# Sliding-window attention and a sentence-level expert layer on one core: gate logits inside the third scores tile, the fallback's transfers on GpSimd, the last output tiles on ScalarE

## The chip, the cores and the metric

The kernel runs on one core of a Trainium2 chip. The core has five engines, each with an instruction stream of its own: TensorE (PE in the profile; its weight loads are shown apart as PEld), VectorE (DVE), ScalarE (ACT), GpSimd (POOL) and SyncE (SP). They meet only through semaphores. Transfers (DMA) are issued from SP, ACT or POOL and run on 16 DMA engines that all queues share; those issued from POOL also change the number type on the way. TensorE writes into PSUM, from which ACT and DVE copy results to the on-chip memory.

The metric is the device time of one launch in microseconds (us), and the number that counts is the median of several runs.

## The reference

Two stages, 8 batches, 8 heads, 576 positions, head size 64, 8 experts of 512 x 1024:

```python
# attention: q, k, v of shape (8, 8, 576, 64)
scores = scale * np.matmul(q, k.transpose(0, 1, 3, 2))
rel = pos[:, None] - pos[None, :]
scores = np.where((rel >= 0) & (rel < 64), scores, -1e9)
attn = np.exp(scores - np.max(scores, axis=-1, keepdims=True))
attn = attn / (np.sum(attn, axis=-1, keepdims=True) + 1e-09)
attn_out = np.matmul(attn, v)
# expert layer on x = attn_out, heads side by side: (8, 576, 512)
logits = x.mean(axis=1) @ w_gate            # one row of 8 logits per batch
e_idx = np.argmax(logits, axis=1)           # one expert per batch
gate_w = softmax(logits)[arange(B), e_idx]
out[b] = gate_w[b] * (np.maximum(x[b] @ w1[e_idx[b]], 0) @ w2[e_idx[b]])
```

Every batch is sent to one expert as a whole, and which one is known only when the whole attention output of that batch has been averaged over its positions. Only then can that expert's weights (2 MB each for w1 and w2 in float32, stored as float16 on chip) be fetched.

## The kernel before

The attention work is cut into 16 units `u` of four heads (two per batch). For a unit, q and k are loaded (`load_qk`, on POOL), turned by TensorE (`transpose_qk`), and the scores are made in three pieces `c` (`scores`: 14 small matmuls at L374 into a PSUM tile `sp`, then one exponential on ACT at L389 into `pt`, then one multiplication with the window's mask on DVE, `mask_out`, L396). `values` multiplies with v (L417), whose two float16 copies `va` and `vb` are made on DVE by `cast_part`: "whole" is the cast of v, "low" and "high" are two shifted copies. The normalised result is `x`; `transpose_x` turns it into `xT` and sums it over positions for the gate.

`gate(b)` runs when batch b's two units are done: a small float32 matmul gives the logits (tile `gl`, L494), and a chain on DVE (copy to `glog`, largest value, its index, clamp to `eidx`, `gnm`) gives the expert's number. POOL loads it into a register (L514) and issues the transfer of w1 (`load_w1`, tile `w1t`, L546) and w2 (`load_w2`, `w2t`, L552). `gate_weight(b)` computes the gate's softmax weight on ACT and DVE.

The expert layer of an older batch runs between: `expert_up` (eight matmuls per tile, L574, tile `php`; ACT writes the ReLU to `hT`, L578) and `expert_down` (L588 for four blocks of 128 rows, L605 for the last 64 rows, tile `pso`; a copy into `ob`, then the transfer to `out`).

All PSUM tiles come from one pool with four buffers of two banks, taken in turn: whoever takes a tile waits until the readers of the tile four before it are done. The order of the work is the order in which the program is written; nothing is reordered. The main loop runs over steps `t` (one unit each, with the expert work of an older batch between its parts, dealt out by `experts(pace)`). At even steps a gate runs. From step 8 on these are called `easy`. At an easy step the order is: scores pieces 0 and 1, some expert work, the cast of v for the next unit, more expert work, gate and weight loads, scores piece 2, `gate_weight`, then the shifted copies of v.

SP issues the transfers of v and of nearly all outputs. At the end, the last block of 128 rows of the last batch is split in two halves: DVE copies one (L594, sent by SP, L596), ACT the other (L595, sent by ACT, L597). The 64-row block of the same batch stands just before it (L611, two transfers by SP, L613).

Behind all that, L886 loads a flag on each of the five engines. If a check of the softmax sums failed, `general` recomputes everything in a slower, safer way; with the inputs here it never runs, so every engine branches over its code (L888) to the closing semaphore waits and the barrier (L916). The branch stands in each engine's own stream, so what an engine has to skip is what `general` would do on that engine. On the path that skips it, each engine also waits for, and advances, the semaphores that `general` would have used.

Of the kernel before, what the change touches and what calls it, by code (L numbers as in the profile page):

```python
# [17 lines left out]
def general(nc, tc, const, psum, vpool, wpool, xpool, xtp, hpool, opool, small, ident,  # L18
# [16 lines left out]
    with tc.For_i(0, B, 1) as bi:  # L35
# [3 lines left out]
        for h in range(H):  # L39
            ld = vpool.tile([128, 4, NST, D], FP32, tag="vn", name="gld")  # L40
            for i, src in enumerate((q, k, v)):
                rows = src[sl, h].squeeze(0)
                nc.sync.dma_start(out=ld[:, i, 0:4, :], in_=rows[0:512].rearrange(
                    "(m p) d -> p m d", p=128))
                nc.sync.dma_start(out=ld[0:64, i, 4, :], in_=rows[512:576])
            nc.sync.dma_start(
                out=ld[0:64, 3, 0:4, :],
# [96 lines left out]
        for m in range(NST):  # L144
            n = 128 if m < 4 else 64
            pso = psum.tile([128, 2, 512], FP32, tag="ps", name="gpso")
            for fb in range(FB):
                nc.tensor.matmul(out=pso[0:n, 0, :], lhsT=hT[:, fb, 128 * m:128 * m + n],
                                 rhs=w2t[:, fb, :], start=(fb == 0), stop=(fb == FB - 1))
            ob = opool.tile([128, Dm], FP32, tag="ob", name="gob")  # L150
            nc.vector.tensor_copy(out=ob[0:n], in_=pso[0:n, 0, :])
            nc.sync.dma_start(out=out[sl, 128 * m:128 * m + n, :].squeeze(0),
                              in_=ob[0:n])
# [3 lines left out]
def kernel(  # L157
# [10 lines left out]
    nc = tc.nc  # L168
# [185 lines left out]

    sp_ps = {}

    def add_outside(u, c):

        sp = psum.tile([128, 2, 512], FP32, tag="ps", name="sp")
        for s in range(2):  # L360
            P(nc.tensor.matmul(
                out=sp[:, s, 0:384], lhsT=ident,
                rhs=outside[:, c].rearrange("p g w -> p (g w)"), start=True, stop=False))
        sp_ps[u, c] = sp

    def scores(u, c, mask=True):
        qT, kT = qt_tiles[u], kt_tiles[u]
        masked = (u, c) in sp_ps
# [16 lines left out]
        for g in range(g0, g0 + 6):  # L385
            for s in range(2):
                mm(s, g % 2, g, g, 128 if g < g0 + 5 else 64)
        pt = ptp.tile([128, 2, 384], FP16, tag="pt")
        P(nc.scalar.activation(out=pt, in_=sp[:, :, 0:384], func=AF.Exp, scale=scale))  # L389
        pt_tiles[u, c] = pt  # L390
        if mask and not masked:
            mask_out(u, c)
# [98 lines left out]

    def gate(b):
        gl = psum.tile([128, 2, 512], FP32, tag="ps", name="gl")
        P(nc.tensor.matmul(out=gl[:, 0, 0:E], lhsT=onesf, rhs=gparts[b],  # L494
# [87 lines left out]
    def expert_down(b, mt):  # L582
# [3 lines left out]
        if mt < 4:  # L586
# [4 lines left out]
            if b == B - 1 and mt == 3:  # L591

                oc = opool.tile([128, Dm], FP32, tag="ob", name="oc")
                P(nc.vector.tensor_copy(out=ob[:, 0:256], in_=pso[:, 0, 0:256]))  # L594
                P(nc.scalar.copy(out=oc[:, 0:256], in_=pso[:, 0, 256:512]))  # L595
# [5 lines left out]
        else:  # L601

            for fb in range(FB):
                for hf in range(2):
# [5 lines left out]
                        tile_position=(0, 64 * hf)))  # L610
            P(nc.vector.tensor_copy(out=ob[:, 0:256], in_=pso[:, 0, 0:256]))  # L611
            for hf in range(2):
                P(nc.sync.dma_start(  # L613
                    out=out[b, 512:576, ts(hf, 256)],
# [175 lines left out]
    for t in range(START + 1, NU + LAG):  # L790
# [3 lines left out]
        def next_gate():  # L794
            b = t // 2 - 1
            gate(b)
            load_w1(b)
# [25 lines left out]
        if easy:  # L823
            if ahead:
                cast_part(t + 1, "whole")
            experts(pace)
        if gated:

# [9 lines left out]
        if ahead and t > 5:  # L838
            if gated and not easy:
                cast_part(t + 1, "whole")  # L840
        if not easy:
            experts(pace)
        if on:
            scores(t, 2)
        if gated and on:
# [75 lines left out]
```

## Time and profile before

| | |
|---|---|
| runs | 219.78, 220.29, 221.03 us, median 220.29 us |
| profiled execution | 223.27 us, of which the span from the first to the last instruction is 221.6 us |
| PE busy | 199.5 us (90% of the span) |
| ACT busy, DVE busy, POOL busy | 135.0, 127.1, 40.5 us |
| chain that ended last, by engine | PE 52%, DMA 23%, ACT 12%, DVE 5%, issue 3% |
| moved by DMA | 45.64 MB, mean 206 GB/s |
| TensorE clock granted | 0.982 of full speed over the span |

The profile is taken of one execution, which is longer than the median of the runs. In its rows an engine name with a q (SPq, ACTq, DVEq) is that engine's sequencer: branches, semaphore waits, transfers issued. The bracket at a row's end is the idle time of the engine before it and what ended it. A transfer's DMA share is the mean busy share of the 16 DMA engines, counted over packets, so it can exceed 1 a little.

### The profile page before, as it was taken

To read this page: it belongs to the slowest core of one execution; us is meant where nothing else is said; L and a number is where in the kernel's file an instruction comes from. 1 tells how busy PE (TensorE), PEld (TensorE's weight loads), DVE (VectorE), ACT (ScalarE), POOL (GpSimd) and SP (SyncE) were. 2 spreads that over 40 slices of the span, in tenths; PEclk is the share of its full clock that TensorE was granted. 3 is DMA by queue.
4 is the path that set the end of the run, shared out by engine and by line. 5 is a ranking of instruction groups with operands and counts; after the bars stand their busy time and mean duration, and the time that the engine had idled before them with its cause. 6 is when DMAs were issued, how large, how long until landed. Compare 5 with 4: busy or idle time off the path is not lost.

```text
span 221.6 us, 7005 instructions
## 1 busy us (share of the span) xinstructions
PE 199.5 (90%) x3015; PEld 141.1 (64%) x3018; DVE 127.1 (57%) x308; ACT 135.0 (61%) x222; POOL 40.5 (18%) x70
## 2 busy tenths in 40 slices
PE   7668879999899999999799999999999999999940
PEld 2346657756686768855686568774887579469420
DVE  2437698557876867384737576676749473330120
ACT  2277596964768667957588476957593838217200
POOL 7080182053000900052000700050002000200000
PEclk9997999999999999999999999999999999999996
DMA  5999999999999999999999999999955991798240
GB/s 66 238 247 242 181 128 207 242 247 246 234 229 246 305 230 233 239 291 225 242 231 289 179 234 238 245 259 242 247 138 73 219 263 44 122 237 234 82 137 11
DMA packets 32406, 45.64 MB, mean 206 GB/s; under 512 B 2544, under 2 KB 24816, under 8 KB 32368
## 3 DMA queue, kind: packets, MB, share of 16 engines
q0 software_dynamic: 16192, 26.22, 66.7%
q1 hardware_dynamic: 15232, 18.75, 27.6%
q8 instruction: 25, 0.41, 0.7%
q10 hardware_dynamic: 944, 0.16, 0.4%
q14 instruction: 13, 0.11, 0.2%
HBM read 61.90 MB, written 9.44 MB: 322 GB/s over the span
## 4 chain that ended last, share of the span: by engine, by line
PE 52%; DMA 23%; ACT 12%; DVE 5%; issue 3%; POOL 1%; POOLq 0%; ACTq 0%
PE php L574 24%; DMA w1t<-in_moe_w_dram 18%; PE pso L588 13%; PE tp L334 6%; DMA kn<-in_k_dram 5%; ACT pt L389 4%; ACT xT L462 4%; PE op L417 4%; ACT hT L578 3%; PE pso L605 2%; PE sp L374 1%; PE tp L454 1%; DVE pt L396 1%; DVE va L303 1%; PE gl L494 1%
## 5 line engine op out<-in xcount | busy, mean ns | idle before, releaser
L574 PE MATMUL php<-xT,w1t 128*128 128x288 f16 x512 | 69.6, 287 | 3.8 <-DMA w1t<-in_moe_w_dram 2.6
L578 ACT ACTIVATE hT<-php,gatew 128x576 f16<-128x576 f32 x64 | 46.9, 746 | 28.4 <-PE php L574 28.4
L574 PEld LDWEIGHTS <-w1t 128*128 128x128 f16 x512 | 54.9, 113 | 11.9 <-DMA w1t<-in_moe_w_dram 3.9
L588 PE MATMUL pso<-w2t,hT 128*128 128x512 f16 x256 | 60.2, 380 | 0.5 <-ACT hT L578 0.5
L389 ACT ACTIVATE pt<-sp 128x768 f16<-128x768 f32 x48 | 36.6, 822 | 7.1 <-PE sp L374 7.1
L588 PEld LDWEIGHTS <-hT 128*128 128x128 f16 x256 | 23.3, 98 | 26.6 <-issue 1.7
L303 DVE COPY ob<-pso 128x512 f32<-128x512 f32 x23 | 15.9, 690 | 21.6 <-PE pso L588 21.4
L433 DVE TENSOR_TENSOR x<-op,linv 128x640 f16<-128x640 f32 x32 | 26.4, 825 | 1.1
L396 DVE TENSOR_TENSOR pt<-pt,masks 128x768 f16<-128x768 f16 x42 | 23.0, 556 | 6.3 <-ACT pt L389 5.2
L347 ACT COPY dst<-tp 128x1152 bf16<-128x1152 bf16 x16 | 18.0, 1123 | 10.1 <-PE tp L334 9.9
L462 ACT ACTIVATE xT<-tp 128x576 f16<-128x576 f16 x28 | 17.9, 646 | 8.8 <-PE tp L454 8.8
L546 POOL DMA_DIRECT2D w1t<-in_moe_w_dram x5 | 3.6, 718 | 98.0 <-DVE gatew L525 58.6
L417 PE MATMUL op<-vb,pt 128*64 128x65 f16 x320 | 16.4, 198 | 1.0 <-ACT pt L389 0.5
L417 PEld LDWEIGHTS <-pt 128*64 128x64 f16 x640 | 14.0, 114 | 3.9 <-issue 1.9
L417 PE MATMUL op<-va,pt 128*64 128x65 f16 x320 | 16.2, 198 | 0.0
L374 PE MATMUL sp<-dst 64*64 64x128 bf16 (+1 forms) x672 | 13.8, 213 | 2.1 <-ACT dst L301 0.8
L303 DVE COPY vb<-va 64x1152 f16<-64x1152 f16 (+1 forms) x32 | 15.0, 468 | 0.8 <-ACT va L301 0.3
L486 DVE SCALAR_TENSOR_TENSOR gpart<-wg,pooled,gpart 128x8 f32<-128x8 f32 x21 | 4.8, 227 | 18.2 <-ACT xT L462 18.0
L374 PEld LDWEIGHTS <-dst 64*64 64x64 bf16 x672 | 10.3, 107 | 7.3 <-issue 3.0
L303 DVE CAST va<-vn 128x1152 f16<-128x1152 f32 x15 | 11.6, 776 | 4.9 <-DMA vn<-in_v_dram 4.9
L303 DVE COPY dst<-tp 128x1152 bf16<-128x1152 bf16 x8 | 10.9, 1356 | 4.7 <-PE tp L334 4.6
L544 POOL DMA_DIRECT2D w1t<-in_moe_w_dram x7 | 5.6, 800 | 43.5 <-PE pso L588 20.5
(79 smaller groups left out, 185.5 us busy)
## 6 DMA issues: line engine op xcount, KB each, us to landing
w2t<-in_moe_w_dram POOLq DMA_DIRECT2D x8, 1024.0 KB, 17.2
out_dram<-ob SPq DMA_DIRECT2D x31, 256.0 KB, 8.1
w1t<-in_moe_w_dram POOLq DMA_DIRECT2D x5, 1024.0 KB, 8.7
qn<-in_q_dram POOLq DMA_DIRECT2D x16, 288.0 KB, 13.8
kn<-in_k_dram POOLq DMA_DIRECT2D x16, 288.0 KB, 15.4
w1t<-in_moe_w_dram POOLq DMA_DIRECT2D x5, 512.0 KB, 11.1
out_dram<-ob SPq DMA_DIRECT2D x16, 64.0 KB, 7.6
w1t<-in_moe_w_dram POOLq DMA_DIRECT2D x2, 256.0 KB, 4.4
```

The lines of the kernel that those rows point to most:

```text
L303: P(eng.tensor_copy(out=out, in_=in_))
L334: P(nc.tensor.transpose(out=tp[64 * s:64 * s + 64, ts(t, 128)], in_=src[:, s, ts(t, D)], identity=ident, tile_position=(0, 64 * s)))
L347: P(nc.scalar.copy(out=dst.rearrange("p (x r t) -> p x r t", x=2, t=NT), in_=view))
L374: P(nc.tensor.matmul(out=sp[64 * half:64 * half + 64, s, 64 * (qblk - 6 * c):64 * (qblk - 6 * c) + n], lhsT=kT[64 * s:64 * s + 64, ts(kblk ...
L389: P(nc.scalar.activation(out=pt, in_=sp[:, :, 0:384], func=AF.Exp, scale=scale))
L396: P(nc.vector.tensor_tensor(out=pt, in0=pt, in1=masks[:, c].rearrange("p s g w -> p s (g w)"), op=ALU.mult))
L417: P(nc.tensor.matmul(out=op[64 * half:64 * half + 64, xx, 65 * jj:65 * jj + 65], lhsT=pt[:, s, 64 * (g % 6):64 * (g % 6) + 64], rhs=win, s ...
L433: P(nc.vector.tensor_tensor(out=x[:, :, h0 * D:(h0 + 2) * D].rearrange("p j (x c) -> p x j c", x=2), in0=view[:, :, :, 0:64], in1=li[:, :, ...
L462: P(nc.scalar.activation(out=xT[:, kb, :], in_=tp[:, kl, 0:S], func=AF.Copy, accum_out=pooled[:, b, kb:kb + 1]))
L574: P(nc.tensor.matmul(out=php[:, sc, 0:288], lhsT=w1t[:, kb, cols], rhs=xT[:, kb, ts(sc, 288)], start=(kb == 0), stop=(kb == KB - 1)))
L578: P(nc.scalar.activation(out=hT[:, ft].rearrange("p (sc s) -> p sc s", sc=2), in_=php[:, :, 0:288], func=AF.Relu, scale=gatew[:, b:b + 1]))
L588: P(nc.tensor.matmul(out=pso[:, 0, :], lhsT=hT[:, fb, ts(mt, 128)], rhs=w2t[:, fb, :], start=(fb == 0), stop=(fb == FB - 1)))
```

## The change

There are four edits.

1. In `general`, all transfers of inputs and outputs are issued from GpSimd instead of SyncE. SP's code to be skipped shrinks from 186 instructions to 37 and POOL's grows from 44 to 189 (counted in the built program, waits and register moves included); ACT's stays at 122, DVE's at 359.
2. At the end of the last batch, the copy of the first half of the last block moves from DVE to ACT, which now makes both halves one after the other, and the two transfers of the 64-row block move from SP to ACT.
3. At the easy steps with a unit (t = 8, 10, 12, 14), the matmuls of scores piece 2 (`scores_mm`) go ahead of the gate, and the gate's logits are written into unused columns of the same PSUM tile instead of a tile of their own. The exponential of the piece (`scores_out`) stays behind the gate.
4. At the same steps the "whole" cast of v moves from before the gate to behind the gate's chain.

```diff
--- before.py
+++ after.py
@@ general @@
-                nc.sync.dma_start(out=ld[:, i, 0:4, :], in_=rows[0:512].rearrange(
+                nc.gpsimd.dma_start(out=ld[:, i, 0:4, :], in_=rows[0:512].rearrange(
                     "(m p) d -> p m d", p=128))
-                nc.sync.dma_start(out=ld[0:64, i, 4, :], in_=rows[512:576])
-            nc.sync.dma_start(
+                nc.gpsimd.dma_start(out=ld[0:64, i, 4, :], in_=rows[512:576])
+            nc.gpsimd.dma_start(
                 out=ld[0:64, 3, 0:4, :],
...
-            nc.sync.dma_start(out=out[sl, 128 * m:128 * m + n, :].squeeze(0),
+            nc.gpsimd.dma_start(out=out[sl, 128 * m:128 * m + n, :].squeeze(0),
                               in_=ob[0:n])
@@ scores @@
     def scores(u, c, mask=True):
+        scores_mm(u, c)
+        scores_out(u, c, mask)
+
+    def scores_mm(u, c):
         qT, kT = qt_tiles[u], kt_tiles[u]
...
+
+    def scores_out(u, c, mask=True):
+        sp = sp_ps[u, c]
         pt = ptp.tile([128, 2, 384], FP16, tag="pt")
         P(nc.scalar.activation(out=pt, in_=sp[:, :, 0:384], func=AF.Exp, scale=scale))
         pt_tiles[u, c] = pt
-        if mask and not masked:
+        if mask and (u, c) not in masked_sp:
             mask_out(u, c)
@@ gate @@
-    def gate(b):
-        gl = psum.tile([128, 2, 512], FP32, tag="ps", name="gl")
+    def gate(b, sp=None):
+
+        if sp is not None:
+            gl = sp[:, :, 384:512]
+        else:
+            gl = psum.tile([128, 2, 512], FP32, tag="ps", name="gl")
@@ expert_down @@
-                P(nc.vector.tensor_copy(out=ob[:, 0:256], in_=pso[:, 0, 0:256]))
+                P(nc.scalar.copy(out=ob[:, 0:256], in_=pso[:, 0, 0:256]))
                 P(nc.scalar.copy(out=oc[:, 0:256], in_=pso[:, 0, 256:512]))
                 P(nc.sync.dma_start(out=out[b, ts(mt, 128), 0:256], in_=ob[:, 0:256]))
                 P(nc.scalar.dma_start(out=out[b, ts(mt, 128), 256:512], in_=oc[:, 0:256]))
...
+            queue = nc.scalar if b == B - 1 else nc.sync
             for hf in range(2):
-                P(nc.sync.dma_start(
+                P(queue.dma_start(
                     out=out[b, 512:576, ts(hf, 256)],
                     in_=ob[64 * hf:64 * hf + 64, 0:256]))
@@ main loop @@
-            gate(b)
+            gate(b, sp_ps[t, 2] if easy and on else None)
...
         if easy:
-            if ahead:
-                cast_part(t + 1, "whole")
             experts(pace)
+            if on:
+                scores_mm(t, 2)
         if gated:
 
             next_gate()
...
         if ahead and t > 5:
-            if gated and not easy:
+            if gated:
                 cast_part(t + 1, "whole")
         if not easy:
             experts(pace)
         if on:
-            scores(t, 2)
+            if not easy:
+                scores_mm(t, 2)
+            scores_out(t, 2)
```

The listings below give the built instruction order, with the semaphores each row waits for in brackets.

DVE at the gate of step 8, before: the masks of pieces 0 and 1 (L396), the cast of v (`va`), the gate's chain from `glog` to `gnm`, the mask of piece 2.

```order
L396 TENSOR_TENSOR pt<-pt,masks 128x768 [waits Activation_49] x2
L303 COPY va_120<-vn 128x18x64
L499 COPY glog<-gl 128x8 [waits PE_49]
L503 MAX gmx<-glog 128x8 [waits DVE_49]
L505 MAX_INDEX graw<-gmx,glog 128x8 [waits DVE_49]
L506 TENSOR_SCALAR eidx<-graw 128x8 [waits DVE_49]
L509 TENSOR_SCALAR gnm<-gmx 128x1
L396 TENSOR_TENSOR pt<-pt,masks 128x768 [waits Activation_49]
L525 RECIPROCAL gatew<-gsum 128x1 [waits Activation_49]
```

The same place now:

```order
L405 TENSOR_TENSOR pt<-pt,masks 128x768 [waits Activation_49] x2
L512 COPY glog<-sp 128x8 [waits PE_49]
L516 MAX gmx<-glog 128x8 [waits DVE_49]
L518 MAX_INDEX graw<-gmx,glog 128x8 [waits DVE_49]
L519 TENSOR_SCALAR eidx<-graw 128x8 [waits DVE_49]
L522 TENSOR_SCALAR gnm<-gmx 128x1
L303 COPY va_120<-vn 128x18x64
L405 TENSOR_TENSOR pt<-pt,masks 128x768 [waits Activation_49]
L538 RECIPROCAL gatew<-gsum 128x1 [waits Activation_49]
```

The cast has moved behind `gnm`, and `glog` is read from the scores tile `sp`. 

TensorE at the same place, before (`php` is the last `expert_up` tile ahead of the gate, `gl` the logits, `sp` scores piece 2, of whose 14 matmuls the first stands here, `pso` the `expert_down` tile behind):

```order
L574 MATMUL php<-xT_1289,w1t_1593 128x288
L494 MATMUL gl<-gpart_1796,onesf 128x8 [waits DVE_49,Activation_49]
L374 LDWEIGHTS dst
L374 MATMUL sp<-dst 64x64 [waits Activation_49]
...
L588 LDWEIGHTS hT_1848 [waits DMASW3_49]
L588 MATMUL pso<-w2t_1594,hT_1848 128x512 [waits Activation_49]
```

And now:

```order
L587 MATMUL php<-xT_1289,w1t_1593 128x288
L380 LDWEIGHTS dst
L380 MATMUL sp<-dst 64x64 [waits Activation_49]
...
L507 MATMUL sp<-gpart_1796,onesf 128x8 [waits DVE_49]
L601 LDWEIGHTS hT_1848 [waits DMASW3_49]
L601 MATMUL pso<-w2t_1594,hT_1848 128x512 [waits Activation_49]
```

The scores piece now comes first, and three tiles are taken where four were, so each tile behind gets the buffer that its predecessor had. On ACT the order is unchanged there, but the exponential of piece 2 now waits for DVE (the read of `glog` in its tile) where it waited for PE.

ACT at the end of the program, before (the ReLU copies of the last batch, the copies of output blocks, the last transfer, the flag, the branch):

```order
L578 ACTIVATE hT_4102<-php,gatew 128x576 x8
L301 COPY ob<-pso 128x512
L595 COPY oc<-pso 128x256
L597 DMA out_dram<-oc 128x256
L886 TENSOR_LOAD okf
L888 COMPARE_AND_BRANCH
```

And now:

```order
L591 ACTIVATE hT_4098<-php,gatew 128x576 x8
L301 COPY ob<-pso 128x512
L628 DMA out_dram<-ob 64x256 x2
L607 COPY ob<-pso 128x256
L608 COPY oc<-pso 128x256
L610 DMA out_dram<-oc 128x256
L903 TENSOR_LOAD okf
L905 COMPARE_AND_BRANCH
```

The two transfers of the 64-row block and the first half's copy stand ahead of the second half's copy on ACT. SP at the end, before: its last transfers, the flag, the branch, and the first rows of `general`'s loop body, of which more than a hundred follow:

```order
L613 DMA out_dram<-ob 64x256 x2
L596 DMA out_dram<-ob 128x256
L886 TENSOR_LOAD okf
L888 COMPARE_AND_BRANCH
L35 COMPARE_AND_BRANCH
L35 UNCONDITIONAL_BRANCH x2
L916 BRANCH_PREFETCH_HINT
L35 ISA
L43 DMA gld<-in_q_dram 128x4x64
L45 ISA
L45 DMA gld<-in_q_dram 64x64
```

On SP the two transfers are gone now, and behind its branch the loop body of `general` is nearly empty:

```order
L613 DMA out_dram<-ob 128x512 x4
L609 DMA out_dram<-ob 128x256
L903 TENSOR_LOAD okf
L905 COMPARE_AND_BRANCH
L35 COMPARE_AND_BRANCH
L35 UNCONDITIONAL_BRANCH x2
L933 BRANCH_PREFETCH_HINT
L35 REGISTER_ALU
L35 COMPARE_AND_BRANCH
L35 UNCONDITIONAL_BRANCH
L905 UNCONDITIONAL_BRANCH
```

With `general` using no transfer of SP any more, the eight waits on SP's transfer semaphores on the skipping path (L888) are gone as well; POOL waits for all eight of its own transfer semaphores on that path, where it waited for two.

More of the change, by code (lines that the diff above doesn't have):

```diff
@@ L355 @@
     sp_ps = {}
+    masked_sp = set()
     def add_outside(u, c):
@@ L364, in add_outside @@
         sp_ps[u, c] = sp
+        masked_sp.add((u, c))
     def scores(u, c, mask=True):
+        scores_mm(u, c)
+        scores_out(u, c, mask)
+    def scores_mm(u, c):
         qT, kT = qt_tiles[u], kt_tiles[u]
```

## The prediction

> **What bounds the kernel now.** I read the page first, then the wait lists, then the last 12 us, then one of the gates.
>
> ```profile
> span 221.6 us, 7005 instructions
> PE 199.5 (90%) x3015; PEld 141.1 (64%) x3018; DVE 127.1 (57%) x308; ACT 135.0 (61%) x222; POOL 40.5 (18%) x70
> ```
>
> TensorE is busy for 90% of the span, so of the 22 us left the question is which end late on a path that the change touches. The wait lists name two kinds: TensorE waiting for w1 or for ACT, and SP waiting for itself at the branch over `general`.
>
> ```profile
> PE php L574 <- DMA w1t<-in_moe_w_dram: 2.6, 4, 1.2
> PE pso L588 <- ACT hT L578: 0.5, 2, 0.3
> PE php L574 <- ACT hT L578: 0.5, 2, 0.3
> SPq L888 <- SPq L888: 3.9, 1, 3.9
> ```
>
> The end in order of time (start, length, engine, what):
>
> ```profile
> 211.37 0.42 DVE L611 COPY ob<-pso 128x256 f32<-128x256 f32 x1 [0.31 <-PE pso L605]
> 211.82 2.31 SPq L613 DMA_DIRECT2D out_dram<-ob  x2
> 213.19 0.42 DVE L594 COPY ob<-pso 128x256 f32<-128x256 f32 x1 [1.40 <-PE pso L588]
> 213.65 0.37 ACT L595 COPY oc<-pso 128x256 f32<-128x256 f32 x1 [4.43 <-DVE ob L594]
> 214.06 0.37 ACTq L597 DMA_DIRECT2D out_dram<-oc  x1
> 214.22 0.55 SPq L596 DMA_DIRECT2D out_dram<-ob  x1
> ```
>
> TensorE is done just before 213.19, and the span ends at 221.6: 8.4 us of closing work. The rows by line of the flag, the branch (with the waits behind it) and the closing waits, and the landing time of L597's transfer, say what fills them (lengths in ns, then first and last start):
>
> ```profile
> L886 SPq TENSOR_LOAD <-okf x1: 604/604/604, 214.8 to 214.8; - x1
> L888 SPq COMPARE_BRANCH  x1: 50/50/50, 215.5 to 215.5; - x1
> L888 SPq EVENT_SEMAPHORE  x8: 17/17/17, 219.4 to 219.9; - x8
> L888 ACTq COMPARE_BRANCH  x1: 45/45/45, 215.0 to 215.0; - x1
> L888 ACTq EVENT_SEMAPHORE  x1: 17/17/17, 215.5 to 215.5; - x1
> L888 DVEq COMPARE_BRANCH  x1: 62/62/62, 213.8 to 213.8; - x1
> L888 DVEq EVENT_SEMAPHORE  x1: 21/21/21, 216.9 to 216.9; - x1
> L888 POOLq INC_SWDGE_SEM  x1: 1232/1232/1232, 192.1 to 192.1; - x1
> L916 SPq EVENT_SEMAPHORE  x14: 17/28/28, 220.0 to 221.6; - x14
> L916 POOLq DRAIN  x3: 46/107/13458, 193.3 to 221.4; - x3
> DMA to landing us min/median/max: 2.7/2.7/2.7
> ```
>
> SP leaves its branch 3.9 us after taking it (215.5 to 219.4), although the last output landed near 214.06 + 2.7 = 216.8 us (L596's a little later). ACT, whose code to skip is shorter (122 instructions against SP's 186), needs 0.5 us; DVE, with 359, needs 3.1. So the span is ended by SP getting over code that doesn't run, and not by the outputs.
>
> The gate of step 8, from the chain that ended last, then TensorE, ACT and one row of DVE there:
>
> ```profile
> 93.54 0.56 DVE pt L396
> 94.10 0.67 DVE va L303
> 96.22 0.39 issue
> 96.62 10.17 DMA w1t<-in_moe_w_dram
> ...
> 93.14 0.28 PE L494 MATMUL gl<-gpart,onesf 128*128 128x8 f32 x2
> 93.56 0.36 PE L374 MATMUL sp<-dst 64*64 64x64 bf16 x14
> 94.19 1.89 PE L588 MATMUL pso<-w2t,hT 128*128 128x512 f16 x8 [0.27 <-ACT hT L578]
> ...
> 91.99 1.52 ACT L389 ACTIVATE pt<-sp 128x768 f16<-128x768 f32 x2
> 93.37 1.40 ACT L578 ACTIVATE hT<-php,gatew 128x576 f16<-128x576 f32 x2
> 94.62 0.86 ACT L389 ACTIVATE pt<-sp 128x768 f16<-128x768 f32 x1
> ...
> 96.13 0.91 DVE L303 COPY vb<-va 64x1152 f16<-64x1152 f16 x2
> ```
>
> The cast `va` stands 0.67 us inside the gate's chain, with the logits ready since 93.42. TensorE stops twice: scores piece 2 starts at 93.56, just after the second exponential (to 93.51) frees its buffer, and `pso` starts at 94.19, after the first `hT`.
>
> **The change part by part.**
>
> *Transfers of `general` on POOL.* Nothing that runs is moved; SP's skip falls from 186 to 37 instructions. The nearest row is ACT's: 0.5 us instead of 3.9. The other end is that nothing changes (3.9). I take 0.5, since ACT skips three times as much in that time. The eight L888 waits (219.4 to 220.0) also leave SP. POOL takes over the long skip at about 191 us; by the rows of DVE and SP that costs it 3 to 4 us there, and its closing DRAIN lasted until 193.3 + 13.5 = 206.8 anyway. Its one INC_SWDGE_SEM of 1.23 us served two semaphores and now serves eight: between 1.23 and 4 x 1.23 = 4.9 us, so even started at 206.8 it ends by 211.7. Cost nothing, covered by TensorE's work until 213.2.
>
> [...]
>
> *The end on ACT.* The two halves now follow each other: 213.19 + 0.37 = 213.56, + 0.37 = 213.93; L595's issue follows its copy by 0.04, so 213.97, and with 2.7 us to land 216.7. SP sends the first half from 213.56: 0.55 for the issue at most, 0.60 for the flag, 0.5 for the branch, 215.2; it is early and waits for the landing. Behind the wait that covers this transfer stand about half of the 14 closing steps; these take 1.6 us in all (220.0 to 221.6), and I take 1.2. The span ends at 217.9: **3.7 us less**. DVE, free of L594, begins its flag at about 211.8 and is over its branch by 211.8 + 0.6 + 3.1 = 215.5, still covered. If SP's stall stays: 213.56 + 0.55 + 0.60 + 3.9 = 218.6, + 1.6 = 220.2, only 1.4 less.
>
> ACT's two transfers of the 64-row block are new in front of its copies. Their waits end with L611 at 211.8. The pair took 2.31 us on SP here, but the row over all batches says otherwise:
>
> ```profile
> L613 SPq DMA_DIRECT2D out_dram<-ob x16: 472/592/1786, 70.1 to 212.3; - x16
> ```
>
> At the median, 2 x 0.59 = 1.2 us, ACT is free at 213.0, ahead of the pso's end: nothing. At 2.31 it is free at 214.1, 0.9 late, and the end term is 2.8. I take the median, because ACT has sent nothing before them, where SP sends all the other outputs.
>
> *Logits in the scores tile.* With one buffer less taken, scores piece 2 gets the buffer of the first exponential (done by 92.8) and `pso` that of the second (93.51). Both stops go: 93.56 - 93.42 = 0.14, plus 0.27, is 0.4 us of TensorE per gate, at four gates (the four waits of 0.27 are the two rows for `hT`). The logits' matmul comes 0.36 us later, at about 93.8, still ahead of DVE's being free at 94.10. The exponential of piece 2 now waits for DVE's `glog` copy at about 94.3; ACT is busy until 94.77, so nothing.
>
> *The cast behind the chain.* w1 is asked for 0.67 us earlier. The cast ends at about 95.6 where the mask of piece 2 began at 95.5: 0.1 us, covered by the 1.89 us of `pso` that TensorE has ahead of the values.
>
> What of this reaches the end? These rows decide (TensorE's waits for w1 at batches 3 and 5; then per stretch: busy time of the engines, clock, DMA share, GB/s):
>
> ```profile
> 106.83 0.43 PE L574 MATMUL php<-xT,w1t 128*128 128x288 f16 x2 [1.18 <-DMA w1t<-in_moe_w_dram]
> 154.80 0.43 PE L574 MATMUL php<-xT,w1t 128*128 128x288 f16 x2 [0.37 <-DMA w1t<-in_moe_w_dram]
> ...
> 97.00:107.00 10.00, 8.82 (x134) 5.05 (x129) 6.45 (x15) 6.09 (x10) 3.96 (x7) 1.00 1.09 246
> 146.00:155.00 9.00, 8.63 (x132) 5.07 (x127) 6.12 (x14) 5.97 (x10) 1.60 (x3) 1.00 1.06 225
> 164.00:169.00 5.00, 4.59 (x89) 4.05 (x86) 4.71 (x14) 4.09 (x8) 1.43 (x2) 1.00 0.02 4
> ```
>
> At step 8 the DMA engines are full while w1 comes (1.09), so an earlier request only queues longer, and TensorE's 0.4 us turns into a longer wait at 106.8. At steps 10 and 12 TensorE gains 0.8 us and meets the wait at 154.8: kept is what w1 lands earlier, between 0 (engines full, 1.06) and 0.8 + 0.37, all of it. I take 0.5, nearer to the full engines. At step 14 the DMA engines are idle (0.02) and TensorE is the bound: the 0.4 us passes through to the last gate and to the end. Sum **0.9 us**, ends 0.4 and 1.6; 0 if the earlier request is lost as well as step 14's gain.
>
> [...]
>
> **The sum.** 221.6 - 3.7 - 0.9 = 217.0 for the span. The profiled execution took 223.27 with 1.7 around the span, and lies 3.0 above the median of the runs; taking the 4.6 us off the median, 220.29 - 4.6 = **215.7 us**. 0.5% is 1.1 us, about what a measurement of this kernel can tell from no change.
>
> **Rivals.**
> - SP's stall is not from the length of the skip and stays: 220.29 - 1.4 - 0.9 = 218.0. Chance 0.13. [...]
> - The two transfers block ACT for 2.31 us: 220.29 - 2.8 - 0.9 = 216.6. Chance 0.12.
> - The gates give nothing, since the full DMA engines set w1's landing and the rest is absorbed: 220.29 - 3.7 = 216.6. Chance 0.10.
> - No measurable change: SP's stall stays and the gates give nothing, 218.9 and above. Chance 0.08.
> - Slower: POOL, with the long skip and eight semaphores, becomes the last to close. It must end later than SP did, 221.6, that is 14.8 us after its 206.8; the rows give 4.9 at most. From 14.8 us on it decides: if its 13.5 us of DRAIN came wholly behind those 4.9, POOL would end at 225.2 instead of 221.6, which makes 220.29 + 3.6 = 223.9. Chance 0.05.
>
> The forecast has the remaining 0.52, with a range of its own of 214.6 to 216.5. The whole range: down to 214.5 (3.7 + 1.6 and 0.5 for the runs' scatter), up to 218.4 (the first rival and the scatter). Faster by over 0.5%: 0.52 + 0.13 + 0.12 + 0.10 = 0.87.
>
> **What would show it.** Right: SP's wait for itself at the branch is below 1 us and the closing waits follow the landing of the last half; TensorE's four waits of 0.27 for `hT` are gone and `glog` follows the second mask directly; the w1 wait of batch 3 grows. Wrong: SP's 3.9 us stays, ACT's copies begin after 213.9, or a closing row of POOL stands last.

## The result

The changed kernel takes 220.05 us at the median (218.21 to 223.13) beside 221.61 us (219.78 to 224.21) of the kernel before on the same chips, 22 runs each: a ratio of 0.992 with a 95% interval of 0.9895 to 0.9948. Some executions fall in a slower state of the chip: the ratios here leave them out, the medians don't, and the traces of the kernel before (granted clock 0.982), e2_end_act (0.979) and e15_copies_early64 (0.988) were taken in it. By the ratio the change saves 1.7 us (1.2 to 2.3), where 4.6 us was forecast, and the time lies above the range of 214.5 to 218.4. Its profiled execution took 219.41 us with a span of 217.9.

The page of the changed kernel, its lists of waits for TensorE and SP, and its end in order of time:

```profile
span 217.9 us, 6996 instructions
PE 199.9 (92%) x3018; PEld 139.3 (64%) x3018; DVE 126.3 (58%) x307; ACT 134.9 (62%) x223; POOL 40.5 (19%) x70
...
PE php L587 <- DMA w1t<-in_moe_w_dram: 1.7, 3, 0.9
PE pso L601 <- DVE ob L303: 0.3, 1, 0.3
...
SPq L609 <- ACT oc L608: 3.4, 1, 3.4
SPq L933 <- DMA out_dram<-oc: 2.4, 1, 2.4
```

```profile
209.06 1.90 PE L601 MATMUL pso<-w2t,hT 128*128 128x512 f16 x8
...
209.63 2.33 ACTq L628 DMA_DIRECT2D out_dram<-ob  x2
212.07 0.37 ACT L607 COPY ob<-pso 128x256 f32<-128x256 f32 x1 [5.04 <-DMA out_dram<-ob]
212.34 0.38 ACT L608 COPY oc<-pso 128x256 f32<-128x256 f32 x1
212.47 0.33 SPq L609 DMA_DIRECT2D out_dram<-ob  x1
212.75 0.37 ACTq L610 DMA_DIRECT2D out_dram<-oc  x1
```

TensorE ends at 209.06 + 1.90 = 210.96, and the span 6.9 us later. In the kernel before, the same row was

```profile
211.26 1.90 PE L588 MATMUL pso<-w2t,hT 128*128 128x512 f16 x8
```

so that TensorE ended at 213.16 and the span 8.5 us later. SP no longer waits for itself; it waits for the landing of the last half. But ACT's copies begin 1.1 us after TensorE's end, since the two 64-row transfers hold ACT until 211.96. The rows of the branch, of the closing waits, of these transfers and of the last one (lengths in ns, then first and last start; landing from issue):

```profile
L905 POOLq INC_SWDGE_SEM  x1: 1232/1232/1232, 203.0 to 203.0; - x1
L905 PEldq COMPARE_BRANCH  x1: 4185/4185/4185, 208.8 to 208.8; - x1
L905 SPq COMPARE_BRANCH  x1: 54/54/54, 213.4 to 213.4; - x1
L933 SPq EVENT_SEMAPHORE  x14: 17/28/28, 213.6 to 217.8; - x14
L933 POOLq DRAIN  x3: 46/107/4309, 204.2 to 217.6; - x3
...
L628 ACTq DMA_DIRECT2D out_dram<-ob x2: 545/1144/1743, 209.6 to 210.2; - x2
...
L610 ACTq DMA_DIRECT2D out_dram<-oc x1: 366/366/366, 212.8 to 212.8; - x1
DMA to landing us min/median/max: 3.9/3.9/3.9
```

SP is over its branch 0.2 us after taking it (213.4 to 213.6). POOL's long DRAIN ends at 204.2 + 4.3 = 208.5, well hidden. The last half needs 3.9 us to land instead of 2.7. TensorE's own branch (PEldq) is new to this reading: its sequencer takes it at 208.8, 2.2 us before its last matmul ends, and stays there for 4.2 us.

The gate of step 8, TensorE, DVE and POOL's request for w1:

```profile
91.79 0.36 PE L380 MATMUL sp<-dst 64*64 64x64 bf16 x14
92.08 0.39 PE L507 MATMUL sp<-gpart,onesf 128*128 128x8 f32 x2
92.33 1.89 PE L601 MATMUL pso<-w2t,hT 128*128 128x512 f16 x8
...
93.40 0.75 DVE L303 CAST va<-vn 128x1152 f16<-128x1152 f32 x1
94.56 0.72 POOL L559 DMA_DIRECT2D w1t<-in_moe_w_dram  x1 [18.98 <-PE pso L601]
95.03 0.47 PE L334 MATMUL tp<-ident,kn 128*64 128x128 bf16 x10 [0.82 <-DMA kn<-in_k_dram]
```

The scores piece, the logits and `pso` follow each other without a stop, and the cast stands behind the chain. The cast is over at 94.15, before POOL's request begins at 94.56. Right behind `pso` TensorE waits 0.82 us for `kn`, more than the 0.4 us forecast as its gain here, and a wait that the trace before doesn't have.

### The profile page after: what moved, and what is told of

It is laid out like the page before. It is cut to its first block, busy times and chain, and to the rows that moved or that the text cites. A ratio compares the mean times of both kernels' runs of the same rounds, so it can differ in the third digit from the quotient of the medians.

```text
span 217.9 us, 6996 instructions
## 1 busy us (share of the span) xinstructions
PE 199.9 (92%) x3018; PEld 139.3 (64%) x3018; DVE 126.3 (58%) x307; ACT 134.9 (62%) x223; POOL 40.5 (19%) x70
## 4 chain that ended last, share of the span: by engine, by line
PE 58%; DMA 21%; ACT 8%; DVE 5%; issue 3%; POOL 1%; ACTq 1%; POOLq 0%
PE php L587 24%; PE pso L601 16%; DMA w1t<-in_moe_w_dram 9%; DMA w2t<-in_moe_w_dram 7%; PE tp L334 6%; DMA kn<-in_k_dram 5%; PE op L426 4%; ACT xT L471 3%; PE sp L380 3%; ACT pt L398 2%; PE tp L463 2%; PE pso L618 2%; ACT hT L591 1%; ACTq L628 1%; DVE vb L303 1%
## 5 line engine op out<-in xcount | busy, mean ns | idle before, releaser
L426 PE MATMUL op<-va,pt 128*64 128x65 f16 x320 | 15.7, 195 | 0.0
L301 ACT COPY ob<-pso 128x512 f32<-128x512 f32 x8 | 4.7, 586 | 13.4 <-PE pso L601 13.4
```

The source lines that it names most:

```text
L426: P(nc.tensor.matmul(out=op[64 * half:64 * half + 64, xx, 65 * jj:65 * jj + 65], lhsT=pt[:, s, 64 * (g % 6):64 * (g % 6) + 64], rhs=win, s ...
```

## The experiments

Each ratio is to runs of the kernel before on the same chip. "Tail" is the time from the end of TensorE's last `pso` matmul to the end of the span in the profiled execution: 8.5 us before, 6.9 in the changed kernel. The tail compares better between traces than the span, because the start differs by up to 2.7 us from one execution to another (the first gate's index at 25.45 us in the trace before, 23.84 after, 26.5 in e5_copies). But a tail is one trace: e12_cast keeps the end of the kernel before as it was, and its tail is 7.0 us.

### The edits one by one

**e1_general_pool**, edit 1 alone:

```diff
-                nc.sync.dma_start(out=ld[:, i, 0:4, :], in_=rows[0:512].rearrange(
+                nc.gpsimd.dma_start(out=ld[:, i, 0:4, :], in_=rows[0:512].rearrange(
...
```

> The kernel before with the first edit alone (the fallback's transfers on POOL). Theory 1, the end costs what SP's stall and ACT's blocked transfers cost: SP is over its branch in about 0.15 us instead of 3.9, nothing of the output path changes, the last output lands near 217.1 on the old scale and the span ends near 218.3, 3.2 us earlier: ratio 0.985 to 0.987. Theory 2, the outputs of the last block are late in any case, because they meet the instruction fetches of the other engines' branches: about what the whole change gave, ratio 0.992.

Measured 0.988 [0.984, 0.993], tail 5.0 us. The ratio is nearer to theory 1, but its interval reaches to the other; the tail is what tells, 3.5 us shorter than before and 2.0 shorter than that of e12_cast.

**e2_end_act**, edit 2 alone:

```diff
-                P(nc.vector.tensor_copy(out=ob[:, 0:256], in_=pso[:, 0, 0:256]))
+                P(nc.scalar.copy(out=ob[:, 0:256], in_=pso[:, 0, 0:256]))
...
+            queue = nc.scalar if b == B - 1 else nc.sync
```

> The kernel before with the second edit alone (both half copies and the two 64-row transfers on ACT). Theory 1: the second 64-row transfer holds ACT for about 1.75 us, the copies begin about 1 us after TensorE's end, SP keeps its stall of 3.9 us: within 0.5 us of before, ratio 0.998 to 1.004. Theory 2: also no change, 0.998 to 1.002; but under it ACT's hold costs nothing, so e4 must equal the whole change.

Measured 1.002 [0.998, 1.006], tail 8.0 us. ACT's first half copy waited 5.3 us for ACT's own transfers, and the last half took 3.9 us to land.

**e3_gates**, edits 3 and 4:

```diff
-            gate(b)
+            gate(b, sp_ps[t, 2] if easy and on else None)
...
-            if gated and not easy:
+            if gated:
                 cast_part(t + 1, "whole")
```

> The kernel before with the third and fourth edits alone (logits in the scores tile, scores piece 2 ahead of the gate, the cast behind the chain). The recorded working says 0.9 us less, between 0 and 1.6: ratio 0.993 to 1.000. If the end alone gave the measured 1.7 us, the ratio is 1.000 within 0.002.

Measured 0.995 [0.991, 0.999], tail 8.2 us.

**e4_no_end**, the changed kernel with edit 2 undone:

```diff
-                P(nc.scalar.copy(out=ob[:, 0:256], in_=pso[:, 0, 0:256]))
+                P(nc.vector.tensor_copy(out=ob[:, 0:256], in_=pso[:, 0, 0:256]))
...
-                P(queue.dma_start(
+                P(nc.sync.dma_start(
```

> The changed kernel with the second edit undone (DVE copies the first half, SP sends the 64-row block). Theory 1: about 1.5 us faster than the changed kernel, since ACT is not held ahead of the last copies: ratio to before 0.982 to 0.987. Theory 2: equal to the changed kernel, 0.992.

Measured 218.01 us, 0.985 [0.979, 0.991], tail 5.0 us. So edit 1 is worth some 2.6 us by itself and the gates about 1.1; the end on ACT is worth nothing alone, and in the whole it gives back 1.9 us of the tail (6.9 against 5.0; the two ratios, 0.992 and 0.985, have intervals that overlap a little). SP's stall had hidden that: while SP ended last, a late half cost nothing (1.002 in e2_end_act).

### Which half of edit 2

**e5_copies** moves the transfers back to SP; **e6_sends** moves the first copy back to DVE instead:

```diff
-            queue = nc.scalar if b == B - 1 else nc.sync
...
-                P(queue.dma_start(
+                P(nc.sync.dma_start(
```

```diff
-                P(nc.scalar.copy(out=ob[:, 0:256], in_=pso[:, 0, 0:256]))
+                P(nc.vector.tensor_copy(out=ob[:, 0:256], in_=pso[:, 0, 0:256]))
```

> The changed kernel, with the two transfers of the 64-row block moved back to SP; both half copies stay on ACT. Theory A (the sends block): what costs is that ACT has to issue the two 64-row transfers ahead of its copies. Without them ACT is free when TensorE ends, the two copies follow each other as DVE's and ACT's did (0.37 + 0.37 against 0.42 + 0.37), and the last half lands 2.5 to 2.7 us after its issue: about 5.0 us from TensorE's end to the end of the span, a ratio of 0.985, as for the change without this edit. Theory B (the copies cost): ACT's copies are late or long by themselves, and the ratio stays at 0.992 with 6.9 us from TensorE's end to the end.

> The changed kernel, with the copy of the first half moved back to DVE; the two transfers of the 64-row block stay on ACT. Theory A: ACT still issues the two transfers for 2.3 us, so the copy of the second half begins about 1.1 us after TensorE's end and its transfer after it; DVE's half is early, which gains nothing, since both halves are needed: 6.5 to 6.9 us behind TensorE, a ratio of 0.991 to 0.993. Theory B: with DVE's copy back, 5.0 us and 0.985.

e5_copies: 217.56 us, 0.979 [0.974, 0.985], tail 4.9 us: the lowest ratio of the versions that still hold `general`, and faster than both kernels. e6_sends: 0.986 [0.980, 0.991], tail 5.6 us; ACT's copy of the second half began 1.0 us after TensorE's end. The copies cost nothing on ACT, and the transfers hold it up: theory A. The time of e6 is missed, though, and is nearer to theory B's 0.985: the last half landed in 2.3 us there and not in 3.9, so that the late copy is only a part of what the transfers cost on ACT.

### The code of `general`

**e7_no_general** and **e8_no_general_no_end** are the changed kernel and e4_no_end without these lines:

```diff
-    fine = nc.values_load(okf[0:1, 0:1], min_val=0, max_val=1,
-                          skip_runtime_bounds_check_because="a comparison's 0 or 1")
-    with tc.If(fine < 1):
-        general(nc, tc, const, psum, vpool, wpool, xpool, xtp, hpool, opool, small, ident,
-                identh, wg, q, k, v, w1e, w2e, out)
```

> The changed kernel without general, its flag's load and the branch (left out: the second computation for inputs whose flag is 0; the result for these inputs doesn't need it). Theory C (fetches): the second 64-row transfer's issue takes 1.7 us and the last half 3.9 us to land because the engines' code for general is fetched over the same DMA engines in that stretch. Without that code the second issue takes the median of 0.59, ACT is free when TensorE ends, and the last half lands in 2.7 or less: 4.6 us behind TensorE, a ratio of 0.983, and within 0.3 us of the same kernel with the end on DVE and SP. Theory D (the issue is long by itself, being the second of a pair of 64-row transfers at the end): 1.7 us stays, the copies begin about 1 us late, 5.7 us behind TensorE, a ratio of 0.988.

> The change without its edit of the end, and without general, its flag's load and the branch (left out: the second computation for inputs whose flag is 0). Both theories: the copies at TensorE's end, the last half issued 0.9 us later and landed 2.5 us after that, then 1.2 us of closing waits: 4.6 us behind TensorE, a ratio of 0.983. Theory C: SP's second 64-row issue falls from 1.65 to 0.59; theory D: it stays at 1.65.

The same two transfers and the last half in e7_no_general:

```profile
L628 ACTq DMA_DIRECT2D out_dram<-ob x2: 536/570/603, 210.2 to 210.8; - x2
DMA to landing us min/median/max: 2.0/2.0/2.1
...
L610 ACTq DMA_DIRECT2D out_dram<-oc x1: 365/365/365, 212.3 to 212.3; - x1
DMA to landing us min/median/max: 1.8/1.8/1.8
```

e7 measured 0.976 [0.970, 0.981] with a tail of 3.8 us, e8 0.980 [0.975, 0.985] with 3.9. Without the code the second issue takes 0.60 us instead of 1.74 and the last half lands in 1.8 us instead of 3.9: theory C, and theory D falls. With that, the end on ACT is as good as the other.

### Which fetch

**e9_shift** and **e10_copies_shift** make TensorE's program 40 instructions longer at its start, in the changed kernel and in e5_copies:

```diff
...
-    busy(13)
+    busy(33, 200)
```

> The changed kernel with its 13 warm-up matmuls of 512 columns at the start cut into 33 of 200 columns: the same columns, and 40 more TensorE instructions in front of everything else. TensorE's code is fetched in pieces of 16 KB, the last one before the branch at 209.9 us, some 10 instructions before TensorE's end; 210 instructions take about 14.5 us there, so 40 more should bring that fetch some 2.8 us earlier, to about 207, ahead of the 64-row block's transfers. Theory C (the fetch's place makes the end long): the second 64-row issue falls from 1.74 to 0.6, both copies begin when TensorE ends, and from TensorE's end to the end of the span it takes 4.8 to 5.5 us instead of 6.9 (the fetch behind the branch stays); ratio 0.982 to 0.987 against 0.992. Theory D (it is not the place of the fetch): 1.74 and 6.9 us stay, 0.992.

> The same 33 warm-up matmuls in the kernel with the transfers of the 64-row block on SP and both half copies on ACT. There ACT's copies were on time already, so theory C expects less: SP's second 64-row issue from 2.0 to 0.6, the other landings up to 2 us earlier, 4.3 to 4.8 us from TensorE's end to the end of the span (4.8 before): a ratio of 0.978 to 0.982. Theory D: no difference to the kernel without it, 0.979 to 0.985.

Measured 0.999 [0.995, 1.003], tail 7.2 us, and 0.992 [0.989, 0.995], tail 5.1 us: both slower than without the edit. In e9_shift ACT's first half copy still waits for ACT's own transfers, 5.2 us against 5.0 in the changed kernel; in e10_copies_shift it waits for TensorE, as in e5_copies. My reading of the last fetch as the next piece of a running program was wrong: in the changed kernel it comes 1.1 us after TensorE's branch, and e14_late_branch, below, moves it with the branch. The fetch ahead of that did move, from 194.9 us to between 189.0 and 194.5, into the last batch's w1. The issue of w1 and its landing, and the instruction packet between 186.8 and 194.5 us, in e9_shift:

```profile
L559 POOL DMA_DIRECT2D w1t<-in_moe_w_dram x1: 713/713/713, 185.8 to 185.8; - x1
DMA to landing us min/median/max: 9.4/9.4/9.4
...
q8 instruction: 1, 0.02, 0.8%
```

In the changed kernel this window holds no such packet (q8), w1 is asked for at the same 185.8 and lands in 8.7 us; TensorE's wait for it is 0.5 us there and 1.2 in e9_shift (0.4 and 1.7 in the pair with SP's transfers). In the kernel before, the changed kernel and e5_copies, where no such packet stands beside this load, it lands in 8.7, 8.7 and 8.6 us, in these two in 9.4 and 9.9. So a fetch beside it cost the load 0.7 and 1.3 us. By their ratios the two kernels lost more, some 1.5 and 2.8 us, and what the rest is stays open.

**e14_late_branch** delays TensorE's branch (and its load of the flag, just ahead of it) by a matmul of one column that reads ACT's first half:

```diff
...
+    late = psum.tile([128, 2, 512], FP32, tag="ps", name="late")
+    P(nc.tensor.matmul(out=late[0:1, 0, 0:1], lhsT=last_ob[0][:, 0:1], rhs=onesf[:, 0:1],
+                       start=True, stop=True))
     fine = nc.values_load(okf[0:1, 0:1], min_val=0, max_val=1,
```

> The changed kernel with one more matmul of one column on TensorE behind the last block, which reads ACT's copy of the first half: TensorE reaches the branch only about 0.5 us after its last block instead of 2.2 us before its end. Theory E: the 16 KB fetch follows the branch by 1.0 us and comes about 4 us later than it did; the second 64-row issue falls from 1.74 to 0.6 and the copies begin when TensorE ends. But TensorE's own 4.2 us at the branch now end about 5.2 us after its last block, so with the closing waits it takes 6.0 to 6.5 us from its end to the span's: 0.4 to 0.9 us less than in the changed kernel at most, a ratio of 0.988 to 0.991. Theory F (another engine's fetch, or none, holds up the issue): it stays at 1.7 and the end is later than in the changed kernel, over 7.5 us and 0.995.

Measured 0.990 [0.986, 0.994], tail 6.3 us. Its branch, its two transfers, its last half and SP's longest closing wait:

```profile
L910 PEldq COMPARE_BRANCH  x1: 4125/4125/4125, 212.3 to 212.3; - x1
...
L629 ACTq DMA_DIRECT2D out_dram<-ob x2: 547/574/600, 210.0 to 210.5; - x2
...
L611 ACTq DMA_DIRECT2D out_dram<-oc x1: 365/365/365, 212.0 to 212.0; - x1
DMA to landing us min/median/max: 1.8/1.8/1.8
...
SPq L938 <- PEq L910: 2.5, 1, 2.5
```

And the DMA queues over the 2.3 us from ACT's first 64-row issue on (packets, MB, share of 16 engines), first in the changed kernel, then in e14_late_branch:

```profile
q1 hardware_dynamic: 137, 0.25, 28.6%
q10 hardware_dynamic: 74, 0.06, 11.4%
q8 instruction: 1, 0.02, 4.6%
q14 instruction: 1, 0.01, 0.9%
```

```profile
q1 hardware_dynamic: 144, 0.26, 29.1%
q10 hardware_dynamic: 150, 0.13, 22.5%
q14 instruction: 1, 0.01, 1.8%
```

One instruction packet of 16 KB (q8; 25 of them with 0.41 MB in the whole span) is the difference: 0.046 x 16 x 2.3 = 1.7 us on one DMA engine. In that time ACT's queue (q10) brought out 74 packets instead of 150. With the branch 3.5 us later the packet comes at 213.6 instead of 209.9, which shows that it is TensorE's; the second issue takes 0.60, the copies begin at TensorE's end (211.33 against 211.29) and the last half lands in 1.8: theory E. The price is that TensorE's 4.1 us at the branch now end last, which SP's wait of 2.5 us shows. A smaller instruction packet (q14, 8 KB) stands beside the transfers in both kernels and doesn't hold up the issues in e14_late_branch.

One of the traces parts the fetch from the branch. In e1_general_pool TensorE takes its branch 0.8 us ahead of the pair on SP, as in the kernel before, where the second issue took 1.79 us. But the packet follows 2.0 us after the branch and not 1.0, at 212.0, when both issues are over:

```profile
L613 SPq DMA_DIRECT2D out_dram<-ob x2: 472/530/587, 210.8 to 211.4; - x2
```

The second issue takes 0.59 us. So it is the packet, and not the branch or the flag's load, that makes the issue long. It also means that this kernel's tail owes something to the luck of a late packet.

The packet itself takes 1.7 us in the changed kernel, 1.6 in e14_late_branch with six packets of output in its 1.9 us window (0.051 x 16 x 1.9), and 1.0 beside the load in e9_shift (0.008 x 16 x 7.7). What sets its length, how it holds up a transfer beside it, and why the issuing instruction is held as well, no run here shows.

**e13_early64** and **e15_copies_early64** leave the branch and put the 64-row block ahead of the block mt = 2, in the changed kernel and in e5_copies:

```diff
-                if tail[0] and (halves[0] or len(left) == 1):
+                if tail[0] and (halves[0] or len(left) == (2 if b == B - 1 else 1)):
```

> The changed kernel with the 64-row block of the last batch one block earlier: ahead of the block mt = 2 instead of behind it. Theory E (the fetch that follows TensorE's branch holds up what is issued beside it): ACT's two 64-row transfers are issued some 1.9 us earlier, ahead of the fetch, and take about 0.55 and 0.6; ACT is free when TensorE ends, the copies follow at once, and L610's transfer, issued 0.7 us after TensorE's end, lands 2.0 to 2.7 us later: 4.4 to 5.0 us from TensorE's end to the span's end instead of 6.9, a ratio of 0.982 to 0.986. Theory D (a pair of 64-row transfers at the end is slow wherever it stands): the second issue keeps 1.7, but earlier, so the copies are nearly on time, and the last half still lands in 3.9: 5.8 to 6.2 us and 0.989.

> The kernel with the 64-row block's transfers on SP and both half copies on ACT, and with the 64-row block one block earlier. There the 2.0 us issue held up SP, whose L609 was issued 0.8 us after its copy was done. Theory E: SP's two issues take 0.5 and 0.6, L609 follows its copy at once, the last half lands about 0.7 us earlier behind TensorE: 4.1 to 4.6 us from TensorE's end to the span's (4.8 without it), a ratio of 0.976 to 0.980. The rival, that the landing of the last halves beside the fetch sets the end whatever stands ahead: 4.8 us, 0.979 to 0.984.

e13 measured 0.987 [0.982, 0.992] with a tail of 5.8 us, e15 0.991 [0.988, 0.995], also 5.8. Rows of e13_early64:

```profile
L905 PEldq COMPARE_BRANCH  x1: 3982/3982/3982, 208.3 to 208.3; - x1
...
L628 ACTq DMA_DIRECT2D out_dram<-ob x2: 547/573/599, 208.2 to 208.8; - x2
...
L610 ACTq DMA_DIRECT2D out_dram<-oc x1: 366/366/366, 212.0 to 212.0; - x1
DMA to landing us min/median/max: 3.8/3.8/3.8
```

Half of theory E held: the issues are short (0.60; 0.59 on SP in e15), and the copies begin at TensorE's end. But the last half still lands in 3.8 us in both, so the expected 4.4 to 5.0 and 4.1 to 4.6 us are missed. For e13 the 5.8 us are what theory D had, but not by its way, since its 1.7 us issue is gone; for e15 the rival's 4.8 us is missed too, though its mechanism is the one seen. TensorE's branch is followed by two packets in the kernel before (212.0 and 216.1) and in the changed one (209.9 and 213.8): the second comes 4.1 and 3.9 us after the first. In e13_early64, with 16 large matmuls behind the 64-row block, TensorE's sequencer runs 3.0 us ahead instead of 2.2 (branch at 208.3, end at 211.29), and a fetch at 213.0, 4.7 us behind the branch, fell on the last half. In the changed kernel it is the second packet as well, at 213.8, that stands beside the last half, issued at 212.75.

### The two gate edits apart

**e11_logits** is before with edit 3 alone, **e12_cast** with edit 4 alone:

```diff
...
-            gate(b)
+            gate(b, sp_ps[t, 2] if easy and on else None)
...
```

```diff
-            if ahead:
-                cast_part(t + 1, "whole")
...
-            if gated and not easy:
+            if gated:
                 cast_part(t + 1, "whole")
```

> Before, with edit 3 alone: the third piece's scores and the gate's logits in its tile, the cast of v still ahead of the gate. The working of the prediction: TensorE's waits of 0.27 for hT at the gates go, 0.4 us less of TensorE per gate, but w1 is asked for when it was, so that the waits for w1 at batches 3 and 5 grow by what TensorE gained (to about 1.6 and 1.2) and only step 14's 0.4 us is kept: 0.4 us in all, a ratio of 0.998. The rival, that the gates are bound by TensorE: the waits for w1 stay as they were and 1.1 us is kept, 0.995.

> Before, with edit 4 alone: the cast of v behind the gate's chain, the logits in a tile of their own. The working of the prediction: w1 is asked for 0.67 us earlier; the waits for w1 at batches 3 and 5 fall by up to 0.67 and 0.37 and the 0.27 us waits for hT stay: 0.4 to 1.0 us, a ratio of 0.996 to 0.998. The rival, that the transfers are bound by the DMA engines: w1 lands when it did, and nothing is gained, 1.000.

Measured 1.004 [1.000, 1.007], tail 8.2 us, and 1.001 [0.997, 1.004], tail 7.0 us. TensorE's waits between 70 and 185 us, in e11_logits, e12_cast and e3_gates:

```profile
PE php L587 <- DMA w1t<-in_moe_w_dram: 1.8, 2, 1.1
...
PE pso L601 <- ACT hT L591: 0.3, 1, 0.3
```

```profile
PE php L574 <- DMA w1t<-in_moe_w_dram: 0.9, 1, 0.9
PE tp L334 <- DMA kn<-in_k_dram: 0.6, 1, 0.6
PE pso L588 <- ACT hT L578: 0.5, 2, 0.3
PE php L574 <- ACT hT L578: 0.5, 2, 0.3
```

```profile
PE php L587 <- DMA w1t<-in_moe_w_dram: 1.3, 1, 1.3
PE tp L334 <- DMA kn<-in_k_dram: 0.9, 1, 0.9
```

The waits for `hT` move as the working had it: edit 3 takes them away, all but one of them when it stands alone, and they stay with the cast alone. Neither edit alone is faster, and only the pair is. e11 misses both its forecast of 0.998 and its rival's 0.995; e12's interval holds the upper end of its forecast and its rival's 1.000. The waits for w1 can't be read from one trace: with the gates as before they come to 1.6 us in the kernel before and 2.1 in e1_general_pool, so the 1.8 of e11 shows no growth. Differences of a few tenths of a per cent between the two singles are not settled by these runs.

## Why the prediction was wrong

- *SP's stall at the branch* was right: 3.9 us became 0.2, and the rival that it stays fell. Edit 1 alone shows it with 0.988. The size of the stall is less firm than it looked: over the same code it is 3.6 us in e3_gates and 3.0 in e12_cast. Why SP stalled over 186 instructions and not over 37, no run here shows.
- *POOL at no cost* was right. Its branch took 5.5 us at 189 us, INC_SWDGE_SEM 1.23 us for eight semaphores as for two, and its DRAIN ended at 208.5.
- *The end on ACT* is the step that failed: 3.7 us were forecast for the end, and the tail gained 8.5 - 6.9 = 1.6. The path was as forecast (copies on ACT, then the landing of the last half, then the closing waits), and two terms on it were mis-sized. The pair of 64-row transfers was taken at 1.2 us by the median of all batches and took 2.33, so that the copies were 1.1 us late; and the landing was taken at 2.7 us and took 3.9. Together 2.3 us, about what is missing. The reason given for the median, that ACT has nothing queued before, was beside the point: the long issue isn't SP's backlog but the first packet behind TensorE's branch, and it is as long on ACT (1.74) as on SP (1.65 in e4_no_end, 1.98 in e5_copies). The long landing stands beside the second packet. The rival of a pair at 2.31 us saw half of it and left the landing at 2.7. The row of the kernel before, 2.31 us for this pair at this place against 1.2 elsewhere, already was the place's price; a median over the other places could not speak against it.
- *Closing in 1.2 us* was right: from the last landing at 216.6 to 217.87 it takes 1.25.
- *The gates* were right in size as a pair as far as e3_gates can tell, 1.1 us [0.2, 2.0] against 0.9. The four waits for `hT` went, and one of 0.27 us for `ob` came. The parts of the sum are not shown. The wait for w1 at batch 3 was to grow and is 0.88 us beside 1.18 before, but in the traces that hold both edits it lies anywhere between 0.3 and 1.8 us. The wait for `kn`, a term that the prediction left at nothing, stands with 0.4 to 1.0 us in ten of the thirteen traces with edit 4 and in none of the four without it; e12_cast has it without edit 3, so it is not only edit 3's gain that is spent there. Where it comes from, no run here shows.

Put together, the traces account for the result: 1.6 us of the tail, and from the first gate's index to TensorE's end 187.71 us before and 187.12 now, which is 0.6 less. The sum of 2.2 lies inside the measured 1.2 to 2.3. The kernel before also took 1.3 us more in these runs than the 220.29 from which the forecast was taken off; that part of the distance to 215.7 lies in the runs and in no step of the working.

What stays open: how much of e5_copies' lead (0.979) is luck, such as the place of its code. Its near relatives e10 and e15 gave 0.992 and 0.991, and their waits for w1 are longer (1.7 us at the last batch in e10, 1.8 at the longest in e15, against 1.2 in e5).

## What to carry to other kernels

Code that is only jumped over was not free here: SP stalled 3.9 us over 186 instructions and DVE 3.1 over 359 in the kernel before, POOL 5.5 over 189 in the changed one, and TensorE's skip also sent two 16 KB fetches over the DMA engines just when the last outputs left (209.9 and 213.8 us in the changed kernel), so look at what every engine's branch sets off before moving work at the end of a kernel. Where one occurrence of an instruction is long at the very place in question, take that row and not the median, and find its cause first. Where such a fetch can fall on the end of a kernel, keep transfers off the engine that makes the last copies: here the two on ACT held its copies back by 1.1 us.

## What the runs showed of the hardware

- Time at a taken branch over code that doesn't run: SP 0.2 us over 37 instructions (changed kernel) and 2.8 (e2_end_act) to 3.9 (before) over 186, ACT 0.4 (e2) to 0.5 (changed kernel) over 122, DVE 2.9 (e15) to 3.5 (e5) over 359, POOL 0.5 over 44 (before) and 5.0 (e14) to 5.9 (e1) over 189, TensorE 3.7 (e10) to 4.4 (e12).
- TensorE's sequencer took its branch 2.2 us before its last matmul ended in the kernel before and the changed one and 3.0 in e13 and e15; e14's added matmul held it until 1.0 us after. A 16 KB fetch followed 1.0 us later before, 1.1 in the changed kernel, 1.3 in e14 and 2.0 in e1, and a second one 4.1 and 3.9 us behind the first in the kernel before and the changed one.
- Beside such a fetch the second 64-row issue took 1.79 us on SP (before) and 1.74 on ACT (changed kernel), and without one 0.59 (e1) and 0.60 (e13, e14). A transfer of half a block took 3.9 us (changed kernel) and 3.8 (e13) to land beside one, and 1.8 without (e14); in the kernel before, where the packet came 2.0 us after its issue, 2.7. Without any of that code (e7) the issue took 0.60 us, the landing 1.8, and the tail is 3.8 us, 3.1 below the changed kernel's.
- Forty instructions more at the start of TensorE's program moved a running fetch beside a weight load and cost 0.7 us of waiting there, some 190 us later (1.2 us in e9 against 0.5; 1.3 in the second pair, 1.7 in e10 against 0.4 in e5).
